# Weight conversion in steps of two halves, 1024 columns wide, with high and low pieces in tiles of their own

## The chip, the cores and the metric

One core of a Trainium2 chip runs the program. Its engines work side by side, each through its own instructions in order: PE (TensorE, matmuls), DVE (VectorE), ACT (ScalarE), POOL (GpSimd) and SP (SyncE, which here only issues DMAs). The metric is the device time of one execution in microseconds (us). The kernel before takes 1411.93 us, the median of three runs (1409.56 to 1413.39).

## The reference

```python
x = attention(q, k, v)      # 8 x 8 heads, chunks of 64 keys, head size 64; each chunk for itself
a, b = x @ w1, x @ w2       # 4608 x 512 by 512 x 1024, twice
x = ((a * b) @ w3) @ w_out  # 1024 x 1024, 1024 x 512
h = x @ w_in2               # 512 x 2048
out = (max(h, 0) + alpha * min(h, 0)) @ w_out2
```

## The kernel before

**Numbers.** Every float32 operand of a matmul is held as two pieces, high (`HI`) and low (`LO`), and each product is three matmuls (`PASSES`, line 25). The weights arrive as float64, one 64-bit word for each number, and are converted on the chip. This is the part that changes.

**Conversion.** A half is 512 columns of 128 rows. Each half `i` goes through a load and five steps (lines 168 to 211): `convert_load` (SP, 512 KB into a `raw` tile), `convert_a` (step A, ACT: absolute value of the upper word into `m`), `convert_b` (step B, DVE: two TENSOR_SCALAR, one SCALAR_TENSOR_TENSOR that reads `raw`), `convert_c` (step C, ACT: high piece), `convert_d` (step D, DVE: one TENSOR_SCALAR, one SCALAR_TENSOR_TENSOR into `p`), `convert_e` (step E, DVE: two TENSOR_TENSOR, low piece). That is seven DVE and two ACT instructions for a half. There are 72 halves in the order of `CONVERTED` (line 54): 16 of `w12` (columns of w1 and w2 in turn, eight f's), 8 of `wo`, 16 of `w3t`, 32 of `w2nd`. The `w2nd` halves (`second_weight`) need no C and E, only an addition; every two of them are combined and split into four pieces `wm`, which go to DRAM.

**First stage.** Blocks b of 512 tokens, nine in all. A block's input `x_t[b]` comes from two attention units: S (scores, PE), M (maximum, DVE), X (exponentials, ACT), Y (normalise, DVE), T (transpose, PE), P (copy, ACT), V (values, PE), c and d (high and low piece of x, ACT and DVE). For each b and f, `proj1` runs 12 matmuls into `pa` and 12 into `pb`, ACT copies `pa` into `a`, DVE multiplies, and SP writes `a` to `g_dram`.

The head of this stage, units 0 to 5, blocks 0 and 1 and the conversion of `w12` and `wo`, follows a written list, `STARTUP` (line 37). A letter is a step, the number its half, unit or block and f: `A3` is step A of half 3; `i` and `g` are the first 8 and last 4 matmuls of `pa`, `j` and `h` those of `pb`, `k` the copy, `m` the product. Up to the `|` ACT, DVE and PE keep the list's order. From block 2 on, PE's order is that of the code (`pinned`, line 592). In this loop `convert()` (line 258) is called after each f, and takes one half: a `w3t` half is converted and later multiplied with `wo` (`fold`, 12 matmuls into `wc`), a `w2nd` half goes the way above. The other engines' and SP's order there is set by a scheduler at build time.

**Buffers before.** `raw`: three tiles of one half. `tmp`: seven tiles of one half, shared by `m`, `p`, `a`, `t14`, `t32`, `wf` and later stages. `gs`: three tiles of two halves. Granules `s0` to `s31` hold two halves each; one granule holds the high and low piece of one converted half.

**After the first stage** come two more, in 876 us: the folded matrices with sums of blocks in seven products for eight, and the second layer. Nothing in them is edited but the pool that some of their tiles come from.

Of the kernel before, what the change touches and what calls it, by code (L numbers as in the profile page):

```python
# [18 lines left out]
P = 128  # L19
# [18 lines left out]
    S0 A0 M0 B0 X0.1 S1 D0 X0.0 M1 A1 Y0 C0 X1.1 E0 T0 B1 X1.0 D1 P0 Y1 A2 V0 C1 B2  # L38
    T1 c0 E1 P1 C2 d0 V1 D2 S2 c1 A3 d1 i0.0 A4 M2 S3 B3 X2.0 g0.0 i0.1 M3 C3 D3 X2.1
    j0.0 E2 h0.0 X3.1 E3 j0.1 Y2 X3.0 g0.1 B4 T2 h0.1 P2 Y3 k0.0 V2 C4 m0.0 q4 A5 T3 D4 k0.1 i0.2  # L40
    P3 B5 V3 m0.1 C5 E4 c2 j0.2 c3 D5 A6 g0.2 E5 i1.0 k0.2 d3 q5 A7 h0.2 d2 S5 | m0.2 B7
    j1.0 B6 i1.1 D7 C6 g1.0 C7 D6 h1.0 k1.0 j1.1 m1.0 E6 g1.1 E7 h1.1 k1.1 A8 i0.3 m1.1 A9 B8 i1.2 B9
    j0.3 M5 C9 D9 g0.3 h0.3 k0.3 D8 C8 j1.2 A10 m0.3 X5.0 E8 i1.3 E9 g1.2 A11 B10 h1.2 k1.2 j1.3 m1.2 C10
    D10 g1.3 B11 h1.3 k1.3 i0.4 E10 C11 X5.1 m1.3 S4 D11 A12 j0.4 E11 M4 g0.4 h0.4 k0.4 B12 A13 i1.4 X4.0 m0.4
    B13 i0.5 C12 D13 C13 j1.4 D12 g0.5 E12 g1.4 E13 h1.4 k1.4 A14 j0.5 m1.4 A15 B14 k0.5 i1.5 X4.1 B15 h0.5 D14
    g1.5 m0.5 j1.5 k1.5 D15 C15 C14 Y5 i0.6 E14 h1.5 g0.6 m1.5 j0.6 k0.6 E15 Y4 A16 i1.6 B16 h0.6 j1.6 m0.6 C16
    D16 A17 g1.6 E16 h1.6 k1.6 A18 i0.7 m1.6 B17 T4 D17 j0.7 P4 B18 C17 g0.7 E17 h0.7 k0.7 V4 m0.7 A19 C18
    D18 T5 A20 E18 i1.7 P5 B20 V5 B19 j1.7 c5 d5 g1.7 D19 h1.7 k1.7 C20 m1.7 C19 D20 A21 E19 E20 A22
    B22 A23 B21 D22 C21 c4 B23 D21 C23 C22 D23 d4 E21 E23 E22 q6
# [8 lines left out]
RAW = 3  # L58
# [21 lines left out]
def tile_attention_moe_moe(ctx: ExitStack, tc: tile.TileContext, qkv: bass.AP, w12: bass.AP,  # L80
# [22 lines left out]
    work = ctx.enter_context(tc.tile_pool(name="work", bufs=2))  # L103
    psum = ctx.enter_context(tc.tile_pool(name="psum", bufs=1, space=bass.MemoryType.PSUM))
# [35 lines left out]
    def tmp(name):  # L140
        return work.tile([P, TB], F32, tag="tmp", name=name, bufs=TMP)
# [25 lines left out]

    def convert_load(i):
        if i < len(conv) and i not in conv_raw:
            w, f, half = conv[i]  # L170
            raw = conv_raw[i] = work.tile([P, TB, 2], U32, tag="raw", name="raw", bufs=RAW)
            words = src[w][f][:, TB * half:TB * half + TB].bitcast(U32)
            nc.sync.dma_start(out=raw, in_=words.rearrange("p (n w) -> p n w", w=2))

    def convert_a(i):
        if i >= len(conv) or i in conv_m:
            return
        convert_load(i)
        convert_load(i + 1)
        convert_load(i + 2)  # L180
        w, f, half = conv[i]
        n = 2 * f + half
        if w != "m":
            w_g[w, f, half] = halves("w3") if w == "c" else granule({"a": 8 + n, "o": n}[w], "w" + w)
        conv_m[i] = tmp("m")
        scalar.activation(out=conv_m[i], in_=conv_raw[i][:, :, 1].bitcast(F32), func=AF.Abs)
# [20 lines left out]

    def convert_e(i):
        m, g = conv_m[i], w_g[conv[i]]
        vector.tensor_tensor(out=m, in0=m, in1=g[:, HI].bitcast(F32), op=ALU.subtract)  # L210
        vector.tensor_tensor(out=g[:, LO], in0=m, in1=conv_p[i], op=ALU.add)
# [4 lines left out]
    def second_weight(i):  # L216

        convert_a(i)
        convert_b(i)
        convert_a(i + 1)  # L220
        convert_d(i)
        m = conv_m[i]
        vector.tensor_tensor(out=m, in0=m, in1=conv_p.pop(i), op=ALU.add)

    def combined_weight(i):
# [3 lines left out]
        w0, w1 = conv_m.pop(i - 1), conv_m.pop(i)  # L229
# [9 lines left out]
        t14, t32 = (tmp(n).rearrange("p (g a c) -> p g a c", a=4, c=32) for n in ("t14", "t32"))  # L239
# [792 lines left out]
```

## Time and profile before

| | before |
|---|---|
| median of three runs | 1411.93 us |
| profiled execution | 1412.95 us |
| its span, first to last instruction | 1411.2 us |
| PE busy | 1375.1 us, 97% |
| DVE busy | 1089.9 us, 77% |
| ACT busy | 764.2 us, 54% |
| DMA traffic | 296.71 MB, 210 GB/s |
| granted PE clock, mean | 0.998 |

Outside the span lie 1.75 us. [...]

### The profile page before, as it was taken

The page shows a single profiled execution, that of the slowest core. Times are in us where ns is not written, and L with a number is a line of the kernel's source. Part 1 is how long each engine was busy: PE and PEld are TensorE (multiplying, and loading weights), DVE is VectorE, ACT ScalarE, POOL GpSimd, SP SyncE. Part 2 cuts the span into 40 slices and gives each one's busy share as a digit, 9 for nine tenths or more (in the row PEclk, how much of TensorE's full clock was granted, in tenths as well). Part 3 has the DMA queues.
Part 4 walks back from the last instruction along what each step waited for, and adds up shares of the span by engine and source line. Part 5 has one row for each costly group of instructions (what it writes and reads, how often), then busy time and mean ns, then how long its engine had stood idle before and what let it go on. Part 6 is the DMA issues. An engine that isn't in the chain of part 4 may idle for free.

```text
span 1411.2 us, 23182 instructions
## 1 busy us (share of the span) xinstructions
PE 1375.1 (97%) x8584; PEld 1147.3 (81%) x8584; DVE 1089.9 (77%) x1606; ACT 764.2 (54%) x1596; POOL 9.5 (1%) x22
## 2 busy tenths in 40 slices
PE   5899999999999999999999999999999999999998
PEld 4687788888778889887888888888897888888888
DVE  6798987877978865989856757585657878789786
ACT  5653554464555533554567767686765444444433
POOL 0000000000000000000000000000000000000020
PEclk9999999999999999999999999999999999999999
DMA  8545575789998855666993424242598564736452
GB/s 280 185 164 165 193 265 193 252 286 332 308 317 286 302 208 176 202 232 218 311 326 143 165 107 155 115 149 112 181 332 328 173 203 134 212 132 180 148 151 89
DMA packets 140673, 296.71 MB, mean 210 GB/s; under 512 B 14608, under 2 KB 62224, under 8 KB 140560
## 3 DMA queue, kind: packets, MB, share of 16 engines
q1 hardware_dynamic: 139760, 293.67, 61.0%
q8 instruction: 67, 1.10, 0.3%
q0 software_dynamic: 512, 1.05, 0.2%
q10 hardware_dynamic: 288, 0.52, 0.1%
q14 instruction: 46, 0.38, 0.1%
HBM read 182.98 MB, written 112.20 MB: 209 GB/s over the span
## 4 chain that ended last, share of the span: by engine, by line
PE 83%; DVE 6%; DMA 5%; ACT 3%; issue 1%; SPq 1%; DVEq 0%; ACTq 0%
PE q L126 15%; PE a L126 13%; PE c L126 13%; PE d L126 13%; PE b L126 13%; PE bc L126 10%; PE wc L126 3%; ACT e L72 2%; DVE m L72 1%; PE pa L126 1%; DMA araw<-g_dram 1%; PE pa L131 1%; DVE p L72 1%; DVE op L72 1%; DMA raw<-in_w 1%
## 5 line engine op out<-in xcount | busy, mean ns | idle before, releaser
L126 PE MATMUL q<-op,w 128*128 128x512 f32 (+1 forms) x960 | 212.0, 369 | 0.9 <-DVE u L72 0.9
L126 PEld LDWEIGHTS q<-op,w 128*128 128x128 f32 x960 | 168.5, 189 | 31.1 <-DVE u L72 1.4
L72 ACT CAST op<-araw 128x1024 fp32r<-128x1024 f32 (+1 forms) x120 | 115.4, 967 | 109.5 <-DVE araw L72 36.9
L72 DVE TENSOR_TENSOR op<-araw,op 128x1024 fp32r<-128x1024 f32 (+1 forms) x120 | 132.8, 1111 | 25.3 <-ACT op L72 25.0
L126 PE MATMUL bc<-yo,w 128*128 128x512 f32 (+1 forms) x600 | 132.6, 368 | 0.0
L72 DVE TENSOR_TENSOR op<-sum,op 128x1024 fp32r<-128x1024 f32 (+1 forms) x90 | 100.0, 1112 | 39.7 <-ACT op L72 39.3
L72 ACT CAST op<-sum 128x1024 fp32r<-128x1024 f32 (+1 forms) x90 | 86.9, 967 | 76.0 <-PE q L126 46.1
L126 PEld LDWEIGHTS bc<-yo,w 128*128 128x128 f32 x600 | 105.3, 189 | 18.7
L126 PE MATMUL a<-x,wa 128*128 128x512 f32 x432 | 108.7, 399 | 5.0 <-DVE x L72 3.3
L126 PE MATMUL d<-x,wa 128*128 128x512 f32 x432 | 106.6, 393 | 1.7 <-ACT wa L72 1.7
L126 PE MATMUL b<-x,wa 128*128 128x512 f32 x432 | 106.5, 393 | 0.0
L126 PE MATMUL c<-x,wa 128*128 128x512 f32 x432 | 106.3, 392 | 0.0
L126 PEld LDWEIGHTS a<-x,wa 128*128 128x128 f32 x432 | 81.2, 191 | 23.8 <-DVE x L72 4.6
L72 ACT ACTIVATE e<-sc,mx 128x64 f32<-128x64 f32 x288 | 86.6, 361 | 18.2 <-DVE mx L72 16.6
L126 PEld LDWEIGHTS d<-x,wa 128*128 128x128 f32 x432 | 80.3, 188 | 18.9 <-ACT wa L72 2.1
L126 PEld LDWEIGHTS c<-x,wa 128*128 128x128 f32 x432 | 80.4, 188 | 16.6
L126 PEld LDWEIGHTS b<-x,wa 128*128 128x128 f32 x432 | 80.2, 188 | 16.8
L126 PE MATMUL c<-op,w 128*128 128x512 f32 (+1 forms) x345 | 89.6, 368 | 0.0
L126 PE MATMUL d<-op,w 128*128 128x512 f32 (+1 forms) x345 | 89.6, 368 | 0.0
L126 PE MATMUL a<-op,w 128*128 128x512 f32 (+1 forms) x315 | 82.0, 369 | 1.1 <-DVE op L72 1.1
L126 PE MATMUL b<-op,w 128*128 128x512 f32 (+1 forms) x315 | 81.8, 369 | 0.0
L72 ACT ACTIVATION_READ_ACCUMULATOR e<-sc,mx 128x1 f32 x288 | 71.6, 255 | 0.0
(156 smaller groups left out, 2462.5 us busy)
## 6 DMA issues: line engine op xcount, KB each, us to landing
araw<-g_dram SPq DMA_DIRECT2D x120, 512.0 KB, 4.1
g_dram<-r SPq DMA_DIRECT2D x144, 256.0 KB, 2.0
w_dram<-wm SPq DMA_DIRECT2D x48, 512.0 KB, 4.6
w<-w_dram SPq DMA_DIRECT2D x48, 512.0 KB, 5.9
qk<-in_qkv SPq DMA_DIRECT2D x36, 512.0 KB, 5.8
g_dram<-a SPq DMA_DIRECT2D x72, 256.0 KB, 3.9
raw<-in_w2nd SPq DMA_DIRECT2D x32, 512.0 KB, 5.4
raw<-in_w SPq DMA_DIRECT2D x16, 512.0 KB, 4.6
```

Of the source, the lines that this page charges most:

```text
L72: ins = f(*args, **kw)
L126: ins = nc.tensor.matmul(*args, **kw)
L131: ins = nc.tensor.transpose(*args, **kw)
```

## The change

Halves `i` and `i + 1` of one pair share tiles: `raw` is now two tiles of two halves, `m` two tiles of two halves. The steps take a flag `wide`; with it one instruction covers both halves, 1024 columns. In `STARTUP` a `+` marks such a step (`A4+` covers halves 4 and 5); halves 0 to 3 stay single. The high pieces of a pair lie in one granule and the low pieces in the next. For `w3t` only A and B are wide; for `w2nd` A, B, D and the addition are. Loads run up to four halves ahead, not three. `p` moves to `gs` (for `w3t` to granule 31), `a` gets two buffers of its own, halves of the tile `ex`, and the seven `tmp` of later stages come from a pool that is opened when the conversion's pool is closed. `pieces_out` of `fold` goes round three granules, not four. `STARTUP` is a new list.

```diff
-    S0 A0 M0 B0 X0.1 S1 D0 X0.0 M1 A1 Y0 C0 X1.1 E0 T0 B1 X1.0 D1 P0 Y1 A2 V0 C1 B2
-    T1 c0 E1 P1 C2 d0 V1 D2 S2 c1 A3 d1 i0.0 A4 M2 S3 B3 X2.0 g0.0 i0.1 M3 C3 D3 X2.1
...
+    S0 A0 M0 B0 X0.1 S1 D0 X0.0 M1 A1 Y0 A2 X1.0 B2 T0 D2 X1.1 B1 P0 Y1 A3 V0 C0 B3
+    T1 c0 D1 P1 d0 C1 V1 E0 S2 c1 C3 d1 i0.0 C2 M2 j0.0 D3 X2.0 S3 E1 g0.0 X2.1 E2 i0.1
+    M3 q4 A4+ h0.0 Y2 X3.1 g0.1 B4+ T2 j0.1 P2 k0.0 E3 V2 C4+ m0.0 X3.0 h0.1 D4+ i0.2 c2 Y3 j0.2 k0.1
...
+    passing = ExitStack()
+    conversion = passing.enter_context(tc.tile_pool(name="conversion", bufs=2))
...
     def tmp(name):
-        return work.tile([P, TB], F32, tag="tmp", name=name, bufs=TMP)
+        return pools["later"].tile([P, TB], F32, tag="tmp", name=name, bufs=TMP)
...
+    products_a = work.tile([P, 2, TB], F32, tag="ex", name="a", bufs=1)
+    copies = [0]
+    def copy_a(ps):
+        copies[0] += 1
+        a = products_a[:, copies[0] % 2]
+        scalar.copy(a, ps)
+        return a
...
+    def part(x, i, wide):
+        return x if wide else x[:, i % 2]
...
-            raw = conv_raw[i] = work.tile([P, TB, 2], U32, tag="raw", name="raw", bufs=RAW)
+            pair = conversion.tile([P, 2, TB, 2], U32, tag="raw", name="raw", bufs=2)
...
-    def convert_b(i):
-        m = conv_m[i]
+    def convert_b(i, wide=False):
+        m, raw = part(conv_m[i], i, wide), part(conv_raw[i], i, wide)
...
-    def convert_c(i):
-        scalar.copy(w_g[conv[i]][:, HI], conv_m[i])
+    def convert_c(i, wide=False):
+        scalar.copy(piece(i, wide, HI), part(conv_m[i], i, wide))
+    def spare(name):
+        return work.tile([P, 2, TB], F32, tag="gs", name=name, bufs=3)
+    def convert_d(i, wide=False):
+        if conv[i][0] == "c":
+            conv_p[i] = granule(31, "p", F32)
+        elif i not in conv_p:
+            conv_p[i] = conv_p[i ^ 1] = spare("p")
...
         if conv[i][0] == "m":
-            second_weight(i)
-            if i % 2:
+            if i % 2 == 0:
+                convert_a(i, True)
+                convert_b(i, True)
+            else:
+                convert_a(i + 1, True)
+                second_weights(i - 1)
                 combined_weight(i)
...
     convert_load(1)
+    load_values(0)
     convert_load(2)
-    load_values(0, nc.sync)
+    convert_load(3)
     load_unit(2, False)
...
+    passing.close()
+    pools["later"] = ctx.enter_context(tc.tile_pool(name="later", bufs=1))
```

SP's queue in the first microseconds, before (`qk` and `v` are inputs of attention units, `raw` the weight halves):

```order
L302 DMA qk<-in_qkv 128x1024 x2
L173 DMA raw<-in_w 128x1024
L302 DMA qk<-in_qkv 128x1024 x2
L173 DMA raw<-in_w 128x1024 x2
L310 DMA v<-in_qkv 128x2x128
```

and of the changed kernel:

```order
L339 DMA qk<-in_qkv 128x1024 x2
L190 DMA raw<-in_w 128x1024
L339 DMA qk<-in_qkv 128x1024 x2
L190 DMA raw<-in_w 128x1024
L347 DMA v<-in_qkv 128x2x128
L348 DMA v<-in_qkv 64x2x128
L349 DMA v<-in_qkv 64x2x128
...
L190 DMA raw<-in_w 128x1024 x2
L339 DMA qk<-in_qkv 128x1024 x2
```

The loads of halves 2 and 3 now stand behind the values `v` of unit 0 and ahead of unit 2's `qk`; before, half 2 stood ahead of `v` and half 3 behind all of the values.

PE's order from the first `proj1` on, before (`a` to `d` are the banks of `pa` and `pb`, `sc` scores, the last row a unit's transposes):

```order
L126 MATMUL a<-x,wa 128x512 x8
L126 MATMUL sc<-qk 64x64 x32
L126 MATMUL a<-x,wa 128x512 x4
L126 MATMUL c<-x,wa 128x512 x8
L126 MATMUL b<-x,wa 128x512 x12
L126 MATMUL d<-x,wa 128x512 x8
L126 MATMUL c<-x,wa 128x512 x4
L131 MATMUL pa<-ident,e 128x128 x8
```

and changed:

```order
L126 MATMUL a<-x,wa 128x512 x8
L126 MATMUL b<-x,wa 128x512 x8
L126 MATMUL sc<-qk 64x64 x32
L126 MATMUL a<-x,wa 128x512 x4
L126 MATMUL c<-x,wa 128x512 x8
L126 MATMUL b<-x,wa 128x512 x4
L126 MATMUL c<-x,wa 128x512 x4
L131 MATMUL pa<-ident,e 128x128 x8
```

The first 8 matmuls of `pb` have moved ahead of unit 3's scores, and the 8 into `d` behind unit 2's transposes.

DVE's order from the normalisation of unit 2 (`e<-e,sm`) on, before (`m`, `p` and `wa` belong to the conversion):

```order
L72 TENSOR_TENSOR e<-e,sm 128x1024
L72 TENSOR_SCALAR m<-m 128x512 x2
L72 SCALAR_TENSOR_TENSOR m<-raw,m 128x512
L72 TENSOR_SCALAR sm<-sm 128x16
L72 RECIPROCAL sm<-sm 128x16
```

and changed, from the same instruction on:

```order
L69 TENSOR_TENSOR e<-e,sm 128x1024
L69 TENSOR_SCALAR m<-m 128x1024 x2
L69 SCALAR_TENSOR_TENSOR m<-raw,m 128x1024
L69 TENSOR_TENSOR m<-m,wa 128x512
L69 TENSOR_TENSOR wa<-m,p 128x512
L69 TENSOR_TENSOR a<-b,a 128x512
L69 TENSOR_SCALAR p<-m 128x1024
L69 SCALAR_TENSOR_TENSOR p<-raw,p 128x1024
```

Where step B of one half stood, that of halves 4 and 5 stands, in three instructions of 1024 columns; the last step of half 3 comes after it now.

## Rows read from the trace of the kernel before

**Rows 1.** Windows: stretch, its length, busy us of PE, PEld, DVE, ACT, POOL, clock

```profile
27.26:135.57 108.31, 101.18 (x864) 81.69 (x864) 90.81 (x166) 57.46 (x189) 0.00 (x0) 1.00 0.55 178
135.57:200.00 64.43, 61.98 (x511) 50.29 (x512) 62.98 (x126) 35.42 (x108) 0.00 (x0) 1.00 0.70 235
200.00:320.00 120.00, 120.00 (x964) 98.65 (x957) 90.95 (x176) 59.39 (x197) 0.00 (x0) 1.00 0.69 237
320.00:400.00 80.00, 75.94 (x688) 61.28 (x687) 67.30 (x136) 41.31 (x133) 0.00 (x0) 0.98 0.92 316
535.00:1411.20 876.20, 868.53 (x4221) 733.55 (x4219) 660.80 (x782) 489.50 (x708) 8.82 (x16) 1.00 0.55 188
```

**Rows 2.** Chain that ended last, in order of time: start, duration, what

```profile
86.91 1.09 PE sc L126 x64
...
121.08 0.87 PE pa L131 x8
...
508.84 2.72 PE c L126 x12
```

**Rows 3.** Groups by form, DVE: busy us, mean ns of one, idle before

```profile
L72 DVE SCALAR_TENSOR_TENSOR m<-raw,m 128x512 uint32<-128x512 uint32 x29 | 19.5, 688 | 0.4
L72 DVE TENSOR_SCALAR m<-m 128x512 f32<-128x512 f32 x30 | 12.4, 421 | 4.1 <-ACT m L72 4.0
L72 DVE TENSOR_TENSOR m<-m,wa 128x512 f32<-128x512 f32 x16 | 10.8, 684 | 0.0
L72 DVE TENSOR_TENSOR e<-e,sm 128x1024 f32<-128x1024 f32 x7 | 8.6, 1223 | 0.2
...
L72 DVE TENSOR_TENSOR wm<-m,wm 128x256 fp32r<-128x256 f32 x12 | 5.0, 419 | 0.0
```

**Rows 4.** Timeline of DVE: start, duration, instructions merged

```profile
8.29 0.89 DVE L72 TENSOR_SCALAR m<-m 128x512 f32<-128x512 f32 x2
9.21 0.69 DVE L72 SCALAR_TENSOR_TENSOR m<-raw,m 128x512 uint32<-128x512 uint32 x1
...
40.64 1.23 DVE L72 TENSOR_TENSOR e<-e,sm 128x1024 f32<-128x1024 f32 x1
41.78 0.88 DVE L72 TENSOR_SCALAR m<-m 128x512 f32<-128x512 f32 x2
...
62.53 1.29 DVE L72 TENSOR_TENSOR m<-m,wa 128x512 f32<-128x512 f32 x2
```

**Rows 5.** Timeline of the start, idle time before in brackets

```profile
8.89 1.13 PE L126 MATMUL sc<-qk 64*64 64x64 f32 x32 [2.15 <-DMA qk<-in_qkv]
10.26 1.13 PE L126 MATMUL sc<-qk 64*64 64x64 f32 x32 [0.23 <-DMA qk<-in_qkv]
...
14.03 0.42 ACT L72 ACTIVATE e<-sc,mx 128x64 f32<-128x64 f32 x1
...
27.26 2.11 PE L126 MATMUL a<-x,wa 128*128 128x512 f32 x8 [0.20 <-ACT x L72]
...
29.63 0.17 DVE L72 TENSOR_SCALAR mx<-mx 128x16 f32<-128x16 f32 x1
```

**Rows 6.** Timeline of PE: where it waits up to the fold

```profile
135.57 3.02 PE L126 MATMUL a<-x,wa 128*128 128x512 f32 x12 [1.08 <-DVE x L72]
...
155.90 2.56 PE L126 MATMUL wc<-wo,w 128*128 128x512 f32 x10 [1.26 <-DVE w L72]
```

**Rows 7.** Timeline of PE, DVE and ACT around the seam of blocks 5 and 6

```profile
373.86 1.06 PE L131 MATMUL pa<-ident,e 128*128 128x128 f32 x8 [1.82 <-DVE e L72]
...
383.07 0.43 DVE L72 TENSOR_SCALAR p<-m 128x512 uint32<-128x512 uint32 x1 [1.54 <-DMA g_dram<-a]
...
386.54 0.41 ACT L72 CAST wm<-m 128x256 fp32r<-128x256 f32 x1 [3.95 <-DVE m L72]
...
389.43 4.61 PE L126 MATMUL a<-x,wa 128*128 128x512 f32 x12 [2.24 <-DVE x L72]
```

**Rows 8.** The writes and reads of `g_dram` from 150 to 540 us

```profile
DMA to landing us min/median/max: 2.0/3.8/6.1
```

More of the change, by code (lines that the diff above doesn't have):

```diff
@@ L57 @@
 QUADS = 4
-RAW = 3
 TMP = 7
@@ L166, in tile_attention_moe_moe @@
     conv_raw, conv_m, conv_p = {}, {}, {}
+    def part(x, i, wide):
+        return x if wide else x[:, i % 2]
     def convert_load(i):
-        if i < len(conv) and i not in conv_raw:
-            w, f, half = conv[i]
-            raw = conv_raw[i] = work.tile([P, TB, 2], U32, tag="raw", name="raw", bufs=RAW)
-            words = src[w][f][:, TB * half:TB * half + TB].bitcast(U32)
-            nc.sync.dma_start(out=raw, in_=words.rearrange("p (n w) -> p n w", w=2))
-    def convert_a(i):
+        if i >= len(conv) or i in conv_raw:
+            return
+        pair = conv_raw.get(i ^ 1)
+        if pair is None:
+            pair = conversion.tile([P, 2, TB, 2], U32, tag="raw", name="raw", bufs=2)
+        conv_raw[i] = pair
+        w, f, half = conv[i]
+        words = src[w][f][:, TB * half:TB * half + TB].bitcast(U32)
+        nc.sync.dma_start(out=pair[:, i % 2], in_=words.rearrange("p (n w) -> p n w", w=2))
@@ L176, in convert_a @@
+    def convert_a(i, wide=False):
         if i >= len(conv) or i in conv_m:
             return
[L178 to L186, printed above, removed]
-    def convert_b(i):
-        m = conv_m[i]
+        for k in range(i, i + 4):
+            convert_load(k)
+        n = i - i % 2
+        for k in (i, i + 1) if wide else (i,):
+            conv_m[k] = conv_m.get(k ^ 1)
+            if conv_m[k] is None:
+                conv_m[k] = conversion.tile([P, 2, TB], F32, tag="m", name="m", bufs=2)
+            w, f, half = conv[k]
+            if w == "c":
+                g = halves("w3")
+                w_g[w, f, half] = [g[:, a] for a in (HI, LO)]
+            elif w != "m":
+                if (w, f) not in w_g:
+                    w_g[w, f] = [granule({"a": 8, "o": 0}[w] + 2 * f + a, "w" + w) for a in (HI, LO)]
+                w_g[w, f, half] = [g[:, half] for g in w_g[w, f]]
+        scalar.activation(out=part(conv_m[i], i, wide), in_=part(conv_raw[i], i, wide)[..., 1].bitcast(F32), func=AF.Abs)
@@ L208, in convert_e, with piece @@
[L208 to L211, printed above, removed]
+    def piece(i, wide, which):
+        return w_g[conv[i][:2] if wide else conv[i]][which]
+    def convert_c(i, wide=False):
+        scalar.copy(piece(i, wide, HI), part(conv_m[i], i, wide))
+    def spare(name):
+        return work.tile([P, 2, TB], F32, tag="gs", name=name, bufs=3)
@@ new lines, in convert_d @@
+    def convert_d(i, wide=False):
[3 more added lines that the diff above has]
+            conv_p[i] = conv_p[i ^ 1] = spare("p")
+        m, raw, p = (part(x[i], i, wide) for x in (conv_m, conv_raw, conv_p))
+        vector.tensor_scalar(out=p.bitcast(U32), in0=m.bitcast(U32), scalar1=0xFF800000, scalar2=None,
+                                op0=ALU.bitwise_and)
+        vector.scalar_tensor_tensor(out=p, in0=raw[..., 0], scalar=2.0 ** -52, in1=p, op0=ALU.mult, op1=ALU.mult)
@@ L213, in tile_attention_moe_moe, with convert_e, second_weights @@
+    def convert_e(i, wide=False):
+        m, p = (part(x[i], i, wide) for x in (conv_m, conv_p))
+        vector.tensor_tensor(out=m, in0=m, in1=piece(i, wide, HI).bitcast(F32), op=ALU.subtract)
+        vector.tensor_tensor(out=piece(i, wide, LO), in0=m, in1=p, op=ALU.add)
     ahead, folds = [len(FIRST)], []
     pieces = [0]
[L216 to L223, printed above, removed]
+    def second_weights(i):
+        convert_d(i, True)
+        vector.tensor_tensor(out=conv_m[i], in0=conv_m[i], in1=conv_p[i], op=ALU.add)
@@ L225, in combined_weight @@
     def combined_weight(i):
         _, j, half = conv[i - 1]
-        w0, w1 = conv_m.pop(i - 1), conv_m.pop(i)
+        w0, w1 = (conv_m.pop(i - 1 + k)[:, k] for k in range(2))
         if half:
@@ L434, in slot @@
             return work.tile([P, 2, TB], dtype, tag=place, name=name, bufs=1)
-        return work.tile([P, 2, TB], dtype, tag=place[:-1], name=name, bufs=3)
+        return (work if place[:-1] == "gs" else pools["later"]).tile([P, 2, TB], dtype, tag=place[:-1], name=name, bufs=3)
     weight = {}
@@ L507, in tile_attention_moe_moe @@
     for step in STARTUP.split():
-        kind, rest = step[0], [int(n) for n in step[1:].split(".") if n]
+        kind, whole = step[0], step[-1] == "+"
+        rest = [int(n) for n in step[1:].rstrip("+").split(".") if n]
         n = rest[0] if rest else 0
@@ L528, in tile_attention_moe_moe @@
         elif kind == "k":
-            a = ab[tuple(rest)][2] = tmp("a")
-            scalar.copy(a, ab[tuple(rest)][0])
+            ab[tuple(rest)][2] = copy_a(ab[tuple(rest)][0])
         elif kind in "ij":
```

65 lines of the change are left out of this document (31 added, 34 removed).

## The prediction, made before the changed kernel ran

> **What bounds the kernel now.** I read the windows first. From 535 us on PE is busy 868.5 of 876.2 us [rows 1]; no step there is edited, so whatever the change does, it does before 535 us. Next the pace: twelve matmuls of 512 columns take 2.72 us on the chain, 0.2267 us each, whatever an instruction's own duration says; a unit's scores or values take 1.09 us, its transposes 0.87 [rows 2]. With that pace I asked what each earlier stretch should have taken. From the first `proj1` matmul (27.26 us) to the first of block 2 (135.57 us) [rows 5, 6] the list holds 16 pairs of `pa` and `pb`, 384 matmuls: 87.0 us; three S, four T and four V add 3.3 + 3.5 + 4.4. That is 98.2 of 108.3 us: 10.1 us lost, though PE looks busy for 101.2. The timeline of PE then shows who is late at the end of it: at 135.57 it waits 1.08 us for x, at 155.90 1.26 us for a `w3t` piece [rows 6], in a stretch where DVE is busy 62.98 of 64.43 us [rows 1]. So up to 200 us DVE sets the pace together with PE. From 200 us on it does not, except at one seam: 1.82 us at 373.86 for a unit's normalised scores, 2.24 us at 389.43 for x of block 6, and the next twelve matmuls take 4.61 instead of 2.72 us, in the one window whose granted clock falls below 1.00, to 0.98 [rows 1, 7]. Before 27.26 us PE waits for data and the attention chain.
>
> **What a wide DVE instruction costs.** A half costs DVE three TENSOR_SCALAR at 0.421 us, two SCALAR_TENSOR_TENSOR at 0.688 and two TENSOR_TENSOR at 0.684: 4.01 us, 8.02 for two. With 1024 columns a TENSOR_TENSOR takes 1.223 us [rows 3]; SCALAR_TENSOR_TENSOR reads `raw` at a step of two words and still costs what TENSOR_TENSOR costs, so I give it 1.223 too. A TENSOR_SCALAR of 1024 columns is not in the trace. Its bounds are 0.421 (nothing more than for 512) and 1.223 (one element at a time). At 512 it costs what TENSOR_TENSOR costs at 256 (0.419) [rows 3], so it goes at twice the rate; I take 0.684, what TENSOR_TENSOR takes for half of 1024. A wide pair then costs 3 x 0.684 + 4 x 1.223 = 6.94 us: 1.08 less in busy time. On the path it is less clear. Where the next instruction doesn't depend on the one before, it starts 0.09 us before the other's end (two take 1.29 us, not 1.38; after the 1.23 at 40.64 the next starts at 41.78); where it depends, 0.03 to 0.04 after it (8.29, 9.21) [rows 4]. So a pair saves between 7 x 0.065 = 0.45 us, all overlapped, and 1.3 us, all in one chain. I use -0.09 and +0.04 below.
>
> [...]
>
> **The start, step by step.** SP now issues halves 2 and 3 behind `v` of unit 0. Data lands in pieces of 0.5 MB, 1.37 us apart (8.89 and 10.26) [rows 5]. Behind the second comes half 1 (11.6), `v` (13.0), half 2 (14.4). Step A of half 2 stands on ACT ahead of unit 1's exponentials, so these start at 14.4 + 0.65 = 15.0 instead of 14.03: 1.0 us late, and the first `proj1` matmul at 28.3 instead of 27.26. Everything behind on SP is one piece (1.37 us) later; unit 2's `qk` is needed first at 26 us, so this is hidden.
>
> In return C0 and E0 leave the path of unit 1, and the 8 matmuls `j0.0` fill PE while it waited before. What gates PE next is DVE. Unit 2's maximum ended 2.54 us after the first `proj1` matmul (29.63 + 0.17 against 27.26) [rows 5], so 30.8 now. Behind it on DVE, up to the low piece of halves 4 and 5 (E4+): D3 1.2, E1 1.3, E2 1.3, M3 1.45, Y2 1.65, B4+ 2.7, E3 1.3, a product 0.65, D4+ 1.9, Y3 1.65, d2 1.15, E4+ 2.45; sum 18.7, at 49.5. PE's work up to there (72 matmuls, 16.3 us; S3, S4, T2, T3, V2, V3, 6.1 us) ends at 50.7, so PE doesn't wait. From E4+ to the low piece of 6 and 7 (E6+): two products and `m1.0` 1.85, M4 1.4, d3 1.15, B6+ 2.4, B8+ 2.4, D6+ 1.75, D8+'s first 0.6, E6+ 2.3, small ones 0.4; sum 14.3, at 63.8. PE has the 41 matmuls and S5 ahead of `g0.3` done by 28.3 + 22.4 + 10.4 = 61.1 and waits 2.7 us. After this 271 matmuls (61.4), T4, T5, V4, V5 (3.9) and four changes of shape at 0.23 (0.9) are left: 130.0. DVE's instructions up to x of block 2, counted the same way, end near 120. 130.0 against 135.57 is 5.6; for semaphores in so long a chain I take one off: **-4.6 us**. If half 2 lands 2 us later or each chain is 10% longer, -1; if `g0.3` doesn't wait, -8.
>
> **Blocks 2 to 4.** DVE has ten wide pairs less of 0.45 to 1.3 us to do, and arrives at the fold with 4 to 13 us in hand; the waits of 1.08 and 1.26 us go: **-2.3 us** (0 to -3). What is late next is PE itself.
>
> **Blocks 5 to 8.** A `w2nd` pair costs 6 x (0.421, 0.688, 0.684 as above) 6.6 us before and 3 x 0.684 + 3 x 1.223 = 5.7 after; 3.5 pairs in block 5 make 3.1 us less. The 1.54 us for which `p` waited for a `g_dram` write [rows 7] goes, since `p` no longer shares buffers with `a`. Against it: each instruction in front of a late one is 1.14 long instead of 0.6, and the cast of x still stands behind work that waits for DVE (3.95 us at 386.54) [rows 7]. Of 1.82 + 2.24 + (4.61 - 2.72) = 5.95 us I take a little over half: **-3.4 us** (+6 to -6).
>
> **New waits.** ACT's copy into `a` now waits for the write of the product two f's earlier. A product ends 6.2 us after its f starts, the second next copy starts at 10.9 + 2.7 = 13.6; of these 7.4 us the write takes 3.8, at most 6.1 [rows 8], and up to 1 for its issue. Nothing is late; if it were, the exponentials and casts behind it on ACT would be, and PE only after the 7 us until the bank is used again. `p` of `w3t` in granule 31 waits for the write of a `wm` piece once in each `w2nd` pair between folds, and three granules in place of four make the fourth piece wait for the first; DVE is busy 90.95 of 120 us there [rows 1], but I charge **+0.9 us** (0 to +5).
>
> Sum: -4.6 - 2.3 - 3.4 + 0.9 = -9.4; 1412.95 - 9.4 = 1403.5. The profiled execution is 1.0 above the median, so I say **1403 us**. Its own range is 1397 to 1408.
>
> **Rivals.** *The gain stays in the list.* Between 135 and 535 us the seam waits come back in another place, since the scheduler lays the casts of x behind longer work, and the start gains half: -2.3 - 2.3 + 1.0, 1409 us. For it: PE is at 120.00 of 120 us from 200 to 320 [rows 1] in a list that is written to its pace, and of the two waits after 135 us only the 1.26 us are for a weight [rows 6]. Against it: 10.1 us lost in the start are more than those waits.
>
> *Slower: x is late at the seams.* The one mechanism: the second half of x for the next block stands on ACT behind a cast that waits for DVE or a granule's write, as at 386.54. It costs 2.24 + 1.89 = 4.13 us each time, clock included, and there are six seams into blocks 3 to 8, of which one is lost now. With n of them lost the kernel changes by 4.13 x (n - 1) - 6.9 + 0.9: slower from n = 3, beyond what can be told from n = 4 (+6.4, 1419 us), 1428 with all six. For it: three granules, and steps twice as long. Against it: less work on DVE, and in the changed order the casts of x are not all behind such casts.
>
> *TENSOR_SCALAR of 1024 columns runs at single rate*, so the change doesn't do what it says: 3 x 1.223 + 4 x 1.223 = 8.56 us a pair, more than 8.02. Nine of them lie before E6+, 9 x 0.54 = 4.9 us later; the start gains nothing, the seams lose 2 us each over four blocks: 1418 us.
>
> **How the numbers follow.** The forecast 0.65, the gain that stays in the list 0.20, late x 0.12, single rate 0.03. A change below 0.3%, 4.2 us, can't be told from none. The forecast's range ends at 1408, so nearly all of it, with a little of the first rival, is faster: 0.64; that rival and the rest 0.23; slower 0.13. The range that should hold the time 8 times in 10 takes the forecast and the first rival, and the edge of the second: 1396 to 1414.
>
> **What would show it.** The first `proj1` matmul at 28.3; E6+ near 64 and a wait of PE there; block 2 from 130 to 132; rows of TENSOR_SCALAR 128x1024 at 0.68; no wait of PE for `w` at the fold; the stage's end near 527 in place of 536. It is wrong if ACT or DVE wait long for DMA writes of `wm` or `a`, if PE waits for x at several seams, or if anything after 535 us changes by more than a microsecond.

## The result and the profile after

The changed kernel takes 1431.68 us, the median of four runs (1430.98 to 1432.21); the kernel before takes 1411.20 beside it. The ratio is 1.0144, with a 95% interval of 1.0126 to 1.0161: it is 20 us slower, where I forecast 9 us faster. Every ratio below is to runs of the kernel before that were taken beside the kernel in question, so ratios are compared rather than times. The profiled execution took 1431.6 us, its span is 1429.8.

The page of the kernel after, its first lines:

```profile
span 1429.8 us, 22840 instructions
PE 1382.9 (97%) x8584; PEld 1153.8 (81%) x8584; DVE 1080.3 (76%) x1416; ACT 757.0 (53%) x1552; POOL 9.5 (1%) x22
```

DVE and ACT have less to do than before, 9.6 and 7.2 us less, and still the end is later. The first thing to find is where. Blocks have the same work on PE in both kernels, so the start of each block's first `proj1` matmul on the timeline of PE can be set side by side:

| us | before | after | lost here |
|---|---|---|---|
| first `proj1` matmul | 27.26 | 31.12 | +3.9 |
| block 2 | 135.57 | 136.03 | -3.4 |
| block 3 | 205.73 | 206.31 | +0.1 |
| block 4 | 278.07 | 280.96 | +2.3 |
| block 5 | 334.25 | 342.14 | +5.0 |
| block 6 | 389.43 | 401.07 | +3.7 |
| block 7 | 441.77 | 460.04 | +6.6 |
| block 8 | 492.36 | 513.17 | +2.5 |
| next stage | 535.88 | 556.68 | 0.0 |
| last instruction | 1411.2 | 1429.8 | -2.2 |

So the start ends even, and 20 us are lost between block 3 and block 8, at the seams where one block ends and the next begins. The timeline of PE in the kernel after shows the seams (start, duration, instructions, idle time before and what ended it):

```profile
206.31 3.06 PE L126 MATMUL a<-x,wa 128*128 128x512 f32 x12 [1.13 <-DVE x L69]
...
268.84 1.16 PE L126 MATMUL pa<-pt,v 64*64 64x64 f32 x64 [2.04 <-ACT pt L69]
...
327.39 1.07 PE L131 MATMUL pa<-ident,e 128*128 128x128 f32 x8 [3.34 <-DVE e L69]
328.21 4.58 PE L126 MATMUL a<-x,wa 128*128 128x512 f32 x12
...
383.62 1.94 PE L131 MATMUL pa<-ident,e 128*128 128x128 f32 x8 [3.69 <-ACT m L69]
...
401.07 5.49 PE L126 MATMUL a<-x,wa 128*128 128x512 f32 x12 [2.62 <-DVE x L69]
...
460.04 5.42 PE L126 MATMUL a<-x,wa 128*128 128x512 f32 x12 [4.49 <-DVE x L69]
```

What was one seam before [rows 7] is now four, those into blocks 4 to 7: x, `pt` or the normalised scores `e` come late there. (The row at 383.62 names ACT's step A, but `e` ended on DVE at the same moment, 383.47 us.) Behind the two longest waits for x the next twelve matmuls take 5.4 us and more where 2.72 is the pace [rows 2]; the granted clock there is 0.50 and 0.56 over 6 us, as the last two lines of the next view show. Its other lines, windows of the kernel after, answer to [rows 1]; the columns are the same:

```profile
135.57:200.00 64.43, 62.73 (x517) 51.16 (x516) 50.00 (x81) 29.82 (x96) 0.00 (x0) 1.00 0.57 193
200.00:320.00 120.00, 116.83 (x934) 95.56 (x933) 87.81 (x142) 53.67 (x170) 0.00 (x0) 1.00 0.69 241
320.00:400.00 80.00, 71.42 (x602) 57.53 (x601) 70.31 (x112) 43.31 (x132) 0.00 (x0) 0.96 0.87 294
400.00:470.00 70.00, 63.73 (x555) 51.09 (x556) 59.74 (x92) 32.98 (x102) 0.00 (x0) 0.90 0.84 288
470.00:540.00 70.00, 70.00 (x493) 57.70 (x492) 29.81 (x46) 26.26 (x91) 0.00 (x0) 1.00 0.64 235
535.00:1411.20 876.20, 874.35 (x4195) 736.71 (x4194) 657.22 (x774) 490.06 (x707) 8.82 (x16) 1.00 0.56 188
401.00:407.00 6.00, 5.93 (x32) 4.32 (x36) 5.93 (x9) 1.43 (x3) 0.00 (x0) 0.50 0.70 223
460.00:466.00 6.00, 5.96 (x52) 4.40 (x56) 5.96 (x10) 1.52 (x3) 0.00 (x0) 0.56 0.90 291
```

DVE (the third pair of numbers) has 50.0 us of work from 135 to 200 us, not 62.98, and only 29.8 from 470 to 540; from 320 to 470 it has more than before. The two windows of the kernel before that were not shown yet:

```profile
400.00:470.00 70.00, 70.00 (x672) 57.38 (x671) 57.58 (x115) 38.37 (x135) 0.00 (x0) 1.00 0.87 304
470.00:540.00 70.00, 70.00 (x389) 58.64 (x388) 43.13 (x79) 24.47 (x58) 0.00 (x0) 1.00 0.63 223
```

Work has moved out of the last block into the ones before it. The tile `raw` says which work. Its step A on ACT from 135 us on, before and then after (count, durations in ns, first and last start in us):

```profile
L72 ACT ACTIVATE m<-raw x50: 657/679/796, 136.9 to 495.9; 128x512 f32<-128x512 f32 x50
```

```profile
L69 ACT ACTIVATE m<-raw x23: 1117/1138/1260, 135.3 to 469.6; 128x1024 f32<-128x1024 f32 x23
```

In a stage that is 20 us longer, the last conversion begins 26 us earlier. And step A now waits for its data. ACT's longest waits from 135 to 540 us after (us in all, times, longest):

```profile
ACT m L69 <- DMA raw<-in_w2nd: 51.6, 11, 7.5
...
ACT wm L69 <- DMA w_dram<-wm: 18.0, 14, 4.2
...
ACT wm L69 <- DMA wc_dram<-wm: 10.6, 5, 3.8
```

Before, ACT waited 4.9 us in two pieces for `w2nd`. At the seam into block 6 it looks like this, on SP and on ACT:

```profile
389.05 0.33 SPq L457 DMA_DIRECT2D g_dram<-a  x1
389.42 0.95 SPq L190 DMA_DIRECT2D raw<-in_w2nd  x2
...
397.31 1.12 ACT L69 ACTIVATE m<-raw 128x1024 f32<-128x1024 f32 x1 [7.51 <-DMA raw<-in_w2nd]
398.32 1.01 ACT L69 CAST x<-pa 128x1024 fp32r<-128x1024 f32 x1
```

The load stands on SP behind the write of a product. ACT is held 7.51 us by step A, and the cast of x, which PE waits for, stands right behind it. Into block 7, where PE waits longest, step A stands ahead of the cast of x too, but there it waits, by the trace, for DVE's subtraction into `t`, which still reads an `m`. Into block 4 `pt` (copied at 267.76 us) stands behind pieces `wm` of a folded matrix that wait for DVE:

```profile
454.52 1.15 ACT L69 ACTIVATE m<-raw 128x1024 f32<-128x1024 f32 x1 [4.46 <-DVE t L69]
...
456.34 1.01 ACT L69 CAST x<-pa 128x1024 fp32r<-128x1024 f32 x1
```

```profile
265.76 1.14 ACT L69 CAST wm<-t 128x512 fp32r<-128x512 f32 x2 [2.98 <-DVE t L69]
```

So the step in front differs from seam to seam; in these three it is one of the work on the weights. That is what the trace tells; whether a wait is the cause or only where the lateness shows, it does not tell.

### The profile page after: what moved, and what is told of

Read it like the earlier page. It is cut to its first block, busy times and chain, and to the rows that moved or that the text cites. A ratio compares the mean times of both kernels' runs of the same rounds, so it can differ in the third digit from the quotient of the medians.

```text
span 1429.8 us, 22840 instructions
## 1 busy us (share of the span) xinstructions
PE 1382.9 (97%) x8584; PEld 1153.8 (81%) x8584; DVE 1080.3 (76%) x1416; ACT 757.0 (53%) x1552; POOL 9.5 (1%) x22
## 4 chain that ended last, share of the span: by engine, by line
PE 76%; DVE 9%; DMA 8%; ACT 3%; issue 2%; SPq 2%; DVEq 0%; ACTq 0%
PE q L126 14%; PE a L126 12%; PE c L126 12%; PE b L126 12%; PE d L126 11%; PE bc L126 10%; PE wc L126 2%; DVE m L69 2%; DMA raw<-in_w2nd 2%; ACT e L69 1%; DVE p L69 1%; PE pa L126 1%; DMA araw<-g_dram 1%; DVE op L69 1%; DMA raw<-in_w3t 1%
## 5 line engine op out<-in xcount | busy, mean ns | idle before, releaser
L126 PE MATMUL a<-x,wa 128*128 128x512 f32 x432 | 114.9, 415 | 9.1 <-DVE x L69 8.2
L126 PEld LDWEIGHTS a<-x,wa 128*128 128x128 f32 x432 | 85.0, 200 | 29.3 <-DVE x L69 9.8
L69 ACT ACTIVATE m<-raw 128x1024 f32<-128x1024 f32 (+1 forms) x38 | 42.2, 1110 | 97.0 <-DMA raw<-in_w2nd 51.6
```

What stands on the lines that cost most here:

```text
L69: ins = f(*args, **kw)
L126: ins = nc.tensor.matmul(*args, **kw)
```

## The experiments

Four theories were on the table. **1**: step A comes a call too early for two pair-wide buffers of `raw` and `m`, and blocks ACT. **2**: steps twice as long stand in front of late ones. **3**: DMA writes of granules and of `a` hold ACT. **4**, formed after the first four runs: the conversion has tiles of its own now, nothing holds it back, and the scheduler crowds it into blocks 4 to 7.

**Step A in its own call.**

```diff
             else:
-                convert_a(i + 1, True)
                 second_weights(i - 1)
```

> The changed kernel with one edit: for w2nd, step A of a pair is no longer given out one call early (in the call of the pair before), but in the pair's own call, directly ahead of step B; the loads stay two calls ahead. Theory 1 (step A comes too early for two pair-wide buffers of raw and m, waits for a load or for m on ACT, and the cast of x, the exponentials and pt stand behind it): ACT's wait for raw of w2nd falls from 51.6 us to under 15, PE's waits at the seams after 306 us fall by more than half, and the time comes to 1416 to 1422 us from 1431.7. Theory 2 (wide steps are twice as long in front of late ones on DVE): no more than 3 us better, 1429 to 1433. Theory 3 (three granules for the fold's pieces, and p, t and a in new places, so that DMA writes hold ACT): no change, 1430 to 1433.

1436.22 us, ratio 1.0156 (1.0136 to 1.0176). No theory's range reaches so far, though the kernel before ran 3 us slower beside it. ACT's wait for `raw` falls and PE's waits stay. The line from ACT's waits of this kernel:

```profile
ACT m L69 <- DMA raw<-in_w2nd: 31.0, 11, 4.6
```

PE still waits 9.6 us for x after 300 us, four times. Two fifths of step A's waits went (51.6 to 31.0 us) and nothing was gained: theory 1 fails as written. With 31 us of waiting left the run does not clear the wait itself.

**No loads for the last `w2nd` halves.**

```diff
+        if i >= len(FIRST + FOLDED) + 8:
+            conv_raw[i] = conv_raw[i - 4]
+            return
         pair = conv_raw.get(i ^ 1)
```

> The changed kernel without the loads of the last 24 halves of w2nd: they use the raw tile of the pair two before, so that part of the output is computed from other weights and 12 MB less are read. Theory 1, if it is the load: the 51.6 us of ACT's wait for raw all but go, time 1414 to 1420 us. If it is the buffers of m that hold step A instead: the wait for raw goes, waits for m's readers on DVE take its place, and the time stays above 1425. Theories 2 and 3: above 1427.

1424.19 us, ratio 1.0072 (1.0045 to 1.0099): some 10 us of the 20 (1.0144 less 1.0072 of 1411). So loads are part of it and not all. PE still waits 4.2 us for x into block 5. The result is mixed: the order of ACT changed too, since the scheduler knows of the missing loads. It converts even earlier here: the last step A stands behind 54 copies into `a`, where the changed kernel has 57 (the count is explained below).

**Halves again in `w2nd`.**

```diff
-                convert_a(i, True)
-                convert_b(i, True)
+            convert_a(i)
+            convert_b(i)
+            convert_a(i + 1, ...)
+            convert_d(i)
```

> The changed kernel with steps A, B, D and the addition of w2nd in single halves of 512 columns again, as before, in the same pair-wide tiles. Theory 1: raw and m still come free only by pairs, ACT still waits over 25 us for raw, time 1424 to 1432 us; some gain since a half can start when its own half has landed. Theory 2: the seams are as before, time 1412 to 1418 us. Theory 3: no change, 1429 to 1433 us.

1434.88 us, ratio 1.0153 (1.0125 to 1.0180): as slow as the wide one. Theory 2 fails: the width of an instruction is not what makes x late.

**A shorter lead in the kernel before.**

```diff
         convert_load(i + 1)
-        convert_load(i + 2)
```

> The kernel before with one edit: step A of a half issues the load of the next half only, not of the next two (the three raw tiles stay). Theory 1: ACT's waits for raw after 135 us rise from 14.7 us to 30 or more, x is late at more seams than one, and the time goes from 1411 to 1416 to 1425 us. Theories 2 and 3: a load is still a call ahead of its step, 1409 to 1414 us.

1409.46 us, ratio 0.9970 (0.9953 to 0.9986). By theory 1 it had to be slower; it is a little faster. With loads one half ahead in place of two, the seams into blocks 6 and 7 come at 386.97 and 437.69 us, and PE waits 0.3 us at the first. A short lead alone does no harm.

What the slow kernels share with the changed one is in none of these edits. I counted on ACT, in the order of the built program, how many of the 72 copies into `a` stand ahead of the step A that completes a number of halves (each block has eight copies):

```
halves converted      36   48   56   64   72
before                25   36   45   55   65
after                 24   32   42   49   57
step A in its own call 24  32   42   51   58
halves again          24   32   41   49   57
no last loads         24   32   41   47   54
shorter lead, before  25   36   45   55   65
```

The calls in the code are the same in all of them: the last conversion belongs into block 8. In the changed kernel and its variants it stands one block earlier or more. Halves 49 to 72 take 25 copies where they took 29, and those before are early too. That made theory 4.

**The conversion held to the code's order.** Step A and the copies into `a` keep program order on ACT from block 2 on; nothing else is edited.

```diff
+    def paced(ins):
+        if pinned[0]:
+            tc.keep_in_program_order(ins)
...
-        scalar.copy(a, ps)
+        paced(scalar.copy(a, ps))
...
-        scalar.activation(out=part(conv_m[i], i, wide), ...)
+        paced(scalar.activation(out=part(conv_m[i], i, wide), ...))
```

> The changed kernel with one edit: from block 2 on step A and the copies into a keep the order of the code on ACT, so that the scheduler can't put a conversion ahead of the block that it is called in. In the changed kernel the last step A stands behind 57 of the 72 copies, in the kernel before behind 65; with the edit it is at 63 or 64. Theory 4 (the conversion now has tiles of its own, nothing holds it back to the pace of the blocks, and the scheduler crowds it into blocks 4 to 7, where it stands in front of x, the exponentials and pt): PE's lost time from 306 us on falls from 27 to under 15 us, the time from 1431.7 to 1412 to 1421 us. Theory 1 (step A one call early into two pair-wide buffers): step A still waits for loads, 1427 to 1433 us. Theory 3 (writes and granules): no change.

1416.48 us, ratio 1.0039 (1.0025 to 1.0052): 15 of the 20 us are back. The last step A stands behind 64 copies. Step A's wait is all but gone, in the same pair-wide buffers and with the same call ahead. The line from ACT's waits and two windows of this kernel:

```profile
ACT m L69 <- DMA raw<-in_w2nd: 3.4, 3, 2.0
```

```profile
400.00:470.00 70.00, 70.00 (x614) 57.47 (x613) 56.69 (x88) 37.22 (x132) 0.00 (x0) 1.00 0.86 302
470.00:540.00 70.00, 70.00 (x431) 57.76 (x430) 44.60 (x69) 25.79 (x66) 0.00 (x0) 1.00 0.67 239
```

From 400 us on PE is full again, and DVE has 44.6 us of work in the last window, near the 43.1 of the kernel before. Blocks 5 to 8 begin at 340.99, 395.53, 446.29 and 496.88 us. In this trace block 2 begins at 140.34 us and the next stage at 540.39: 400.1 us, where the kernel before takes 400.3 and the changed one 420.7. So from block 2 on all of the loss is made good, and the 5 us that stay lie before block 2. Of ACT's waits for granule writes, 18.0 and 10.6 us in the changed kernel, 7.0 are left (`wc_dram`), with granules and buffers as they were: theory 3 is not the main cause.

**`a` in tiles of its own, in the kernel before.** One of the parts of the change that free the conversion's tiles from another user (the others, the moves of `p`, `t14`, `t32` and `wf`, were not tried alone):

```diff
-            a = tmp("a")
-            scalar.copy(a, pa)
+            a = copy_a(pa)     # halves of the tile ex, in turn
```

> The kernel before with one part of the change: a gets two buffers of its own (the halves of the ex tile) and leaves the seven tiles that it shared with m, p, t14, t32 and wf. The last step A moves from behind 65 copies to behind some 60. Theory 4: the conversion runs ahead here too, PE waits for x, e or pt at two or more seams, and the time goes from 1411 to 1415 to 1424 us. Theories 1 and 3: no change from this, 1409 to 1413 us. If the two buffers of a hold ACT (its copy waits for the write of a product), 1413 to 1418 with waits of ACT for g_dram writes.

1428.22 us, ratio 1.0126 (1.0104 to 1.0147). This one edit, with narrow steps, the old list and the old loads, costs as much as the whole change but some 3 us, more than theory 4 had said. From its waits of ACT and of PE, from 135 us on:

```profile
ACT m L72 <- DMA raw<-in_w2nd: 37.4, 17, 7.5
```

```profile
PE a L126 <- DVE x L72: 8.5, 3, 3.6
PE pa L126 <- ACT pt L72: 4.4, 3, 3.9
PE pa L131 <- DVE e L72: 3.3, 2, 2.1
```

The last step A stands behind 59 copies, not 65. In this trace half of the loss lies ahead of block 2, which begins at 143.12 us, 7.5 late; from there to the next stage (549.84) the kernel takes 406.7 us, 6.4 more than before. The long wait for `pt` lies in the first part. In front of it is again a step A that waits for its load, here of a `w3t` half (PE, then ACT):

```profile
136.91 1.98 PE L126 MATMUL pa<-pt,v 64*64 64x64 f32 x64 [3.86 <-ACT pt L72]
```

```profile
134.38 0.67 ACT L72 ACTIVATE m<-raw 128x512 f32<-128x512 f32 x1 [2.41 <-DMA raw<-in_w3t]
```

**The same, held to the code's order.** The edit of the paced kernel, on top of this one.

> The kernel with a in tiles of its own, as in the run before this one, and with step A and the copies into a held to the order of the code from block 2 on. The conversions stand where they stood in the kernel before (last step A behind 64 or 65 copies). Theory 4: the loss of the run before goes again, 1408 to 1413 us. If the two buffers of a were what cost, it stays: 1413 to 1420 us.

1410.70 us, ratio 0.9995 (0.9982 to 1.0007). The loss is gone with `a` still in its own two buffers, so in the sum these buffers and their waits for writes (3.2 us of ACT) cost nothing that can be measured. From block 2 on the place of the conversions decides: this trace takes 394.1 us to the next stage (141.19 to 535.25), 12.7 less than the one without the hold. It is even 6.2 less than in the kernel before, and that hides a start that is 5.6 us later. What costs these 5.6 us, in a part where nothing is held, isn't shown.

**The order held, the density not.** This tells crowding from mere disorder: the paced kernel, calling its conversions as densely as the scheduler had placed them.

```diff
-    CONVERSIONS = {4: 7, 5: 7, 6: 6, 7: 6, 8: 2}
+    CONVERSIONS = {4: 10, 5: 9, 6: 9, 7: 0, 8: 0}
```

> The paced kernel with the calls themselves moved: 10, 9 and 9 conversions in blocks 4, 5 and 6 and none in 7 and 8, in place of 7, 7, 6, 6 and 2. The last step A stands behind some 55 copies, where the scheduler had put it in the changed kernel (57), but step A and the copies keep the order of the code. Theory 4 in its own words (the density of the conversions in blocks 4 to 7 makes x, e and pt late): the loss comes back, 1424 to 1436 us, DVE is idle in block 8. If it is not the density but the order that the scheduler makes of it (steps put in front of late work out of turn), pinning alone helps and this stays at 1413 to 1420 us.

1427.47 us, ratio 1.0102 (1.0074 to 1.0129). The loss comes back, 9 us over the paced kernel (1.0102 less 1.0039 of 1411), though not by the same victim. PE, then ACT, of this kernel:

```profile
354.36 5.49 PE L126 MATMUL a<-x,wa 128*128 128x512 f32 x12 [3.37 <-ACT a L69]
...
464.60 5.19 PE L126 MATMUL a<-x,wa 128*128 128x512 f32 x12 [4.63 <-ACT a L69]
```

```profile
347.54 1.14 ACT L69 ACTIVATE m<-raw 128x1024 f32<-128x1024 f32 x1 [6.40 <-DMA raw<-in_w2nd]
...
353.73 0.58 ACT L69 COPY a<-a 128x512 f32<-128x512 f32 x1
...
457.36 0.32 ACT L69 ACTIVATE e<-sc,mx 128x64 f32<-128x64 f32 x1 [6.33 <-DVE mx L69]
```

PE waits for a bank whose copy is late. At the first place the copy stands on ACT behind the early step A, with exponentials and pieces `wm` between; at the second, behind exponentials that had waited 6.33 us for a unit's maximum on DVE. Which instruction pays depends on the order. That one pays goes with how densely and how early the conversions are called; the two change together in this run (the last step A stands behind 55 copies).

**The old load order at the start.** In the changed kernel:

```diff
-    load_values(0)
     convert_load(2)
+    load_values(0)
     convert_load(3)
```

> The changed kernel with the load of half 2 ahead of v of unit 0 again on SP, as before the change. In the profile of the changed kernel that load is issued at 10.36 us and step A of half 2 waits for it until 16.12 us, with unit 1's exponentials behind it. If that load is what delays the start: these exponentials start 2 us earlier or more, the first proj1 matmul comes at 28.5 to 29.2 us in place of 31.12, and the time falls by 1.5 to 3 us, to 1428.5 to 1430.5. If the start's list decides with DVE, the first matmul is early but block 2 is not, and the time stays within 1 us.

1428.20 us, ratio 1.0118 (1.0099 to 1.0138), 3.7 us less than the changed kernel, though the two intervals overlap. The first `proj1` matmul comes at 29.49, but block 2 begins at 136.22, no earlier than in the changed kernel (136.03): in this trace nothing of the gain comes from the start. Neither of its two expectations fits, and what this load costs in the whole isn't settled.

**Paced, with two waits of the start removed.**

```diff
-    load_values(0)
     convert_load(2)
+    load_values(0)
...
-                vector.tensor_scalar_mul(nalpha, alpha_sb, -1.0)
+                tc.keep_in_program_order(nc.vector.tensor_scalar_mul(nalpha, alpha_sb, -1.0))
```

> The paced kernel with two edits at the start: half 2 is loaded ahead of v of unit 0 again, and the DVE instruction that makes nalpha keeps the order of the code, so that it no longer stands at 54.72 us before unit 4's maximum and waits 1.69 us for its load, while ACT holds unit 4's first exponentials and behind them the second cast of x of block 1. Of the 5 us that the paced kernel is behind the kernel before, all lie before block 2 by its trace (PE has lost 34.6 us at block 2 against 30.0). If these two waits make them: PE's 3.52 us wait for x at 57 us goes below 2, the time falls from 1416.5 to 1411 to 1414 us. If the wide steps of the list itself are late on DVE: no more than 1.5 us better, 1415 to 1417.

1411.28 us, ratio 0.9990 (0.9977 to 1.0004): level with the kernel before. The line of PE that had waited 3.52 us in the paced kernel:

```profile
53.73 3.06 PE L126 MATMUL c<-x,wa 128*128 128x512 f32 x12 [1.60 <-ACT x L69]
```

Block 2 begins at 134.95, against 140.34 in the paced kernel. Of these 5.4 us, 1.0 lies ahead of the first `proj1` matmul (28.55 against 29.58). The other 4.4 are this wait, 1.60 us for 3.52, and the twelve matmuls behind it, 3.06 us for 5.49. The two edits were not tried apart here; the load edit alone, in the run before, also took the `nalpha` instruction away from this place.

**Paced, with halves in `w2nd`.** The edit of the narrow kernel above, on the paced one.

> The paced kernel with steps A, B, D and the addition of w2nd in single halves of 512 columns again. It says what the wide instructions bring by themselves once the conversions keep their place: by the durations of the trace a pair of w2nd costs DVE 6.6 us in halves and 5.7 us wide, and each step of ACT half as much at a time. If the wide steps help at the seams: 2 to 4 us slower than paced, 1418 to 1421 us. If their saving is off the path: within 2 us of it, 1414 to 1418. If long steps in front of late ones harm: 2 to 4 us faster, 1412 to 1414.

1419.47 us, ratio 1.0045 (1.0028 to 1.0062), inside the interval of the paced kernel. (By its time it would be 3 us slower, but the kernel before ran 2 us slower beside it.) The wide steps of `w2nd` bring nothing that can be measured, once the conversions keep their place.

**Paced and spread further.**

```diff
-    CONVERSIONS = {4: 7, 5: 7, 6: 6, 7: 6, 8: 2}
+    CONVERSIONS = {4: 6, 5: 6, 6: 5, 7: 5, 8: 6}
```

> The kernel of paced_start with its 28 remaining conversions spread further out: 6, 6, 5, 5 and 6 in blocks 4 to 8, in place of 7, 7, 6, 6 and 2; the last step A stands behind 68 copies instead of 64. In that kernel's trace PE waits 2.0 and 2.7 us (and 1.7 us at a lower pace behind the second) for the normalised scores of a unit in blocks 4 and 5, and from 400 us on it hardly waits. Theory 4, in the other direction: with less conversion in blocks 4 and 5 these waits go, 1405 to 1410 us, faster than both kernels. If what is left there is the fixed cost of the softmax chain and not of the conversions: no change, 1410 to 1413. If block 8 is now too full or the last pieces come late for the next stage: slower, 1413 to 1418.

1413.50 us, ratio 1.0005 (0.9988 to 1.0021). At the seams it does what theory 4 says: from 330 us on PE waits for nothing until the next stage, and block 8 begins at 487.90 us, 3.9 earlier than in the kernel of the start edits (491.76). But block 8 is now full, and the next stage's first sums wait for DVE:

```profile
533.96 0.62 PE L126 MATMUL a<-op,w 128*128 128x256 f32 x3 [2.38 <-DVE op L69]
```

What the seams give is handed back there and behind it. No version was found that beats the kernel before clearly; the shorter lead in the kernel before, 0.3%, is the nearest.

## Why the prediction was wrong

By stretch, first as forecast and then as measured: the start -4.6 and +0.5 us, blocks 2 to 4 -2.3 and +7.4, blocks 5 to 8 -3.4 and +12.9, what follows 0 and -2.2. The +0.9 for new waits has no stretch of its own.

**What bounds the kernel now: right.** Nothing from 535 us on is edited, and that part takes 873.1 us after and 875.3 before. All of the loss lies in the first stage. I had bounded a change behind it by one microsecond; it is 2.2, and to the good.

**A wide DVE instruction: right.** The groups of DVE by form, of the kernel after:

```profile
L69 DVE SCALAR_TENSOR_TENSOR m<-raw,m 128x1024 uint32<-128x1024 uint32 x34 | 41.5, 1220 | 0.5
...
L69 DVE TENSOR_SCALAR m<-m 128x1024 f32<-128x1024 f32 x34 | 23.4, 690 | 29.8 <-ACT m L69 29.8
```

0.690 us against 0.684 taken, 1.220 against 1.223. The rival of the single rate is out. But in `w2nd` the saving was worth nothing that can be measured, as the paced kernels show. What the second row says besides is at its end: DVE sat idle 29.8 us in all ahead of step B, until ACT was done with step A.

**The start: the step on SP's load failed.** I took `v` of unit 0 for one piece of 1.37 us and had step A of half 2 at 14.4 us. The trace after, SP and ACT:

```profile
9.07 0.60 SPq L349 DMA_DIRECT2D v<-in_qkv  x1
10.36 1.87 SPq L190 DMA_DIRECT2D raw<-in_w  x2
...
16.12 0.67 ACT L69 ACTIVATE m<-raw 128x512 f32<-128x512 f32 x1 [2.35 <-DMA raw<-in_w]
16.69 0.29 ACT L69 ACTIVATE e<-sc,mx 128x64 f32<-128x64 f32 x1
```

`v` of a unit is six issues, SP gives them out up to 2.1 us apart (the last two at 7.72 and 9.07), and the load behind them goes out only at 10.36. Unit 1's exponentials start 2.66 us later than before (14.03, [rows 5]), not 1.0; the first matmul comes at 31.12 in place of 28.3. Not all of that is the load's. The six other kernels with the same order of loads have the first matmul between 29.09 and 29.58 us, and with the old order it comes at 27.93 to 29.49. By these, one profile each, the load costs about 1 us, and 1.5 to 2 us of the 31.12 were seen in this one execution only.

In the list behind it I had put 101.7 us from the first matmul to block 2; it took 104.9 (108.3 before). The wait that I placed at `g0.3`, 2.7 us, was 0.86 (at 69.13 us), and another stood where I had none. DVE and then ACT and PE of the kernel after:

```profile
55.02 0.17 DVE L69 TENSOR_SCALAR nalpha<-alpha_sb 128x16 f32<-128x16 f32 x1 [1.02 <-DMA alpha_sb<-in_alpha]
...
55.37 0.31 ACT L69 ACTIVATE e<-sc,mx 128x64 f32<-128x64 f32 x1 [3.63 <-DVE mx L69]
...
56.25 1.01 ACT L69 CAST x<-pa 128x1024 fp32r<-128x1024 f32 x1
...
57.32 3.06 PE L126 MATMUL c<-x,wa 128*128 128x512 f32 x12 [2.33 <-ACT x L69]
```

An instruction of block 5, put forward by the scheduler, waits for a load of 16 columns ahead of a unit's maximum (it stood at 55.17 us in the kernel before too, with a wait of 1.07 us, but no late x behind it); exponentials that the list has later stand ahead of the cast of x. I had read the order of the list and not what the scheduler had laid between its steps. In sum the start changed by +0.5 us (135.57 to 136.03), where I had -4.6.

**Blocks 2 to 4: the waits that I named went, others came.** PE no longer waits for a `w3t` piece at the fold, and DVE's 62.98 us in that window are 50.00, as said. But these blocks end 7.4 us later in relation (0.1 + 2.3 + 5.0), not 2.3 earlier, with waits for `pt` and `e` at 268.84 and 327.39 us, where conversions of later blocks had been put in (halves 37 to 56 stand up to four copies earlier). With the order held, in the paced kernel, these blocks take 200.7 us, where the changed one takes 206.1 and the kernel before 198.7: 5.5 of the 7.4 are back.

**Blocks 5 to 8: here the forecast broke.** -3.4 was said, +12.9 came. The step that failed is the sentence that a stall of 1.54 us goes "since `p` no longer shares buffers with `a`". I counted the sharing of seven tiles by `m`, `p`, `a`, `t14`, `t32` and `wf` as a cost, and did not ask what it held back. It was the brake of the conversion: tiles are given out in the order of the code, so a conversion called in block 6 could not take a tile before the copies ahead of it had given theirs back. The edit of `a` alone releases it in the kernel before (the last step A at 59 copies for 65; 1.0126 of 1411, some 18 us more, of which by the trace about half comes before block 2), and holding step A to the code's order takes back 15 us in the changed kernel and 18 there. That the sharing with `a` is a brake is shown by this edit; what the move of `p` adds to it is not. That it acts through the order in which tiles are given out is how I explain it, and wasn't tried by itself.

**New waits: the place was wrong.** The two buffers of `a` cost nothing in the sum. The three granules of the folded pieces show as 10.6 us of ACT's waits for `wc_dram` in the changed kernel and 7.0 in the paced one. The 18.0 us for `w_dram` belong to the pieces of `w2nd`, which go round four granules as before (6.4 us there); they go with the order. The granules were not tested alone.

**The rivals.** The second, late x at the seams, is what happened. I gave it 0.12, and for four seams 1419 us. Four seams it is, but x is late at two of them alone, `pt` or `e` at the others, and the dearest costs more than the 4.13 us of the one before: 4.5 us of waiting into block 7 and 2.4 more for the twelve matmuls behind it, at a granted clock of 0.56. I had the casts of x behind casts that wait for DVE or a granule's write. A cast that waits for DVE is in front at 265.76 us, ahead of `pt`; the casts of x stood behind step A, which waited once for its load and once for `m`. Against it I had said that in the changed order the casts of x are not all behind such casts. The order said more, had I counted it: the last step A stands behind 57 copies, not 65.

**What stays open.** How much of the crowding acts through the load (10 us went without loads, with another and even earlier order) and how much through DVE's and ACT's own time at the seams isn't settled. Nor is what makes block 2 late in the two kernels in which `a` alone was moved.

## What to carry to other kernels

When an edit gives work buffers of its own, ask what the shared ones held back: count, in the built order, where the background work stands against the steps of the foreground, before and after. With PE full from 400 us on in the paced kernel (70.00 of 70 us in both windows), wide steps of `w2nd` brought nothing that can be measured over halves (ratios 1.0039 and 1.0045); the same work packed closer cost (1.0102), and a few tiles or a pinned instruction can serve as its pace (1.0126 with neither, 0.9995 with the pin, in the kernel with `a` in tiles of its own). And where a wait is large in the trace, move the waiting step before believing in it: two fifths of step A's wait went here for no gain.

## What the runs showed of the hardware

A wait of PE at a seam can cost more than its length. Behind the 1.13 us of idling at 206 us twelve matmuls take 3.06 us, at a granted clock of 1.00. After 2.62 and 4.49 us of idling, at 401 and 460 us, the granted clock was 0.50 and 0.56 for the next 6 us, and the twelve took 5.49 and 5.42 us, 2.4 more each time. After the 3.34 us at 327 us they took 4.58, 1.5 more, and in the kernel before only one seam paid that: 4.61 us after 2.24 [rows 7]. The length of the wait alone does not decide. In the kernel with `a` in tiles of its own a wait of 3.65 us was followed by 3.02, with a granted clock of 1.00 in the window from 306 to 400 us, in which the wait and most of the twelve lie:

```profile
397.79 3.02 PE L126 MATMUL a<-x,wa 128*128 128x512 f32 x12 [3.65 <-DVE x L72]
```
